# Linear attention and a feed-forward layer in one kernel: the keys' sums added up to 64 partitions before they are spread

## The chip, the cores and the metric

The kernel runs on one core of a Trainium2 chip. The metric is the device time of one execution in microseconds, median of three runs. The core has a matrix engine (TensorE, PE in the profile; its weight loads are PEld), a vector engine (VectorE, DVE), a scalar engine (ScalarE, ACT), GpSimd (POOL) and a queue that issues transfers (SP). They run side by side and wait for each other by semaphores. Each works through its own instructions in the order in which they stand in the program.

## The reference

Random-feature attention for 8 batches, 8 heads, 576 tokens and a head size of 64 with 128 features, and after it a feed-forward layer over all 4608 tokens:

```python
def phi(x):
    proj = np.einsum('bhsd,md->bhsm', x, omega)
    sq = np.sum(x * x, axis=-1, keepdims=True) / 2.0
    h = proj - sq
    h = h - np.max(h, axis=-1, keepdims=True)
    return np.exp(h) / np.sqrt(m)
q_p, k_p = (phi(q_s), phi(k_s))
kv = np.einsum('bhsm,bhsd->bhmd', k_p, v)
z = np.sum(k_p, axis=2)
num = np.einsum('bhsm,bhmd->bhsd', q_p, kv)
den = np.einsum('bhsm,bhm->bhs', q_p, z)[..., None] + 1e-06
...
h = x @ w_in            # x: num / den as 4608 x 512; w_in 512 x 2048
g = h - np.tanh(h)
return g @ w_out        # 2048 x 512
```

The change concerns z, the sum of the keys' features over the tokens.

## The kernel before

The work is cut into units. A k unit takes one batch b and one pair of heads c and makes two things: `kvw`, the product of the keys' features with the values, and `zb`, the sums z of both heads, spread over all 128 partitions. A q unit takes one chunk of 256 tokens and one pair of heads and makes the columns x that the feed-forward layer reads. The feed-forward layer runs over 18 chunks of 256 tokens, in steps `ffn_h` (products with w_in, L469, then tanh, subtraction and a split of g, L473 to L476) and `ffn_out` (products with w_out, L487 to L489). Between the steps a `beat` advances every open unit by one stage, up to its next `yield`. Chunks 0 and 1 run together in the first part; from chunk 2 on one chunk follows the other.

Matrix products in fp32 are made from fp32r parts: a number is split into a rounded part (hi) and the rest (lo), and the products of the parts are added in PSUM.

Batches 0 and 1 take another path. The 24 units of batches 2 to 7 go through `k_single`. There the features `pa`, `pm` and `pb` of the keys (4, 1 and 4 blocks of 128 tokens) are split by `split` into `khl` and multiplied with the split values `vhl` (L268) into the PSUM bank `pk`. Beside that, `zsum` (L271) and L291, L292 add up the features on GpSimd in `zs`, with 128 partitions (tokens modulo 128) by 2 heads by 128 features. What is left is the sum over the partitions: a product with a matrix of ones, which also spreads the result over all partitions. The changed lines prepare that product and issue it.

Order of the work: the program is written stage by stage as above, and a scheduler then places the instructions of all engines by simulated times. A small edit can therefore move instructions far from it. Buffers set waits too. `khl` has two buffers, and `zhl` takes one of them; `c1` has one, shared by `zt` in `zsum` and by the tile `c1` of L299 (the profile prints it as `c`); `pk` has one bank.

The transition matters for the prediction. At L605 to L612 the first part of the feed-forward layer ends, its output tiles are stored (L500), and chunk 2 starts as soon as its x is split (L409). Around that place the units of batch 2 run, 5 beats apart. Their names in the order below are `2_0` to `2_3` or, for tiles, the head pair and the pool's number.

Of the kernel before, what the change touches and what calls it, by code (L numbers as in the profile page):

```python
# [8 lines left out]
F32 = mybir.dt.float32  # L9
F32R = mybir.dt.float32r  # L10
# [7 lines left out]
B, H, S, D, M = 8, 8, 576, 64, 128  # L18
NT, DM, DFF = B * S, H * D, 2048
P = 128  # L20
# [11 lines left out]
def favor_attention_ffn(ctx: ExitStack, tc: tile.TileContext, qT, kT, va, vt, omT, w, out):  # L32
# [12 lines left out]
    nc = tc.nc  # L45
# [18 lines left out]
    def bank(kind):  # L64
        tags = mode[kind]
        tags.append(tags.pop(0))
        return tags[-1]

    def att(kind, shape, dtype, name):
        pool, bufs = mode[kind]  # L70
        return pool.tile(shape, dtype, tag=kind, name=name, bufs=bufs)
# [30 lines left out]
    ones = const.tile([P, P], F32R, name="ones")  # L102
# [22 lines left out]
    def split_rows(x, f):  # L125

        copy(mode["hi"], x[0:D, 0, :], f[0:D])
        copy(mode["hi"], x[D:P, 1, :], f[D:P])
        nc.vector.tensor_sub(x[D:P, 0, :], f[0:D], x[0:D, 0, :].bitcast(F32))
        nc.vector.tensor_sub(x[0:D, 1, :], f[D:P], x[D:P, 1, :].bitcast(F32))  # L130

    def features(lhs, name):

        n = len(lhs)
        ph = att("phi", [P, 4, M], F32, f"phi_{name}")
        nb = sb.tile([P, 4], F32, tag="nb", name=f"nb_{name}", bufs=12)

        for g in range(0, n, 2):
            m = min(2, n - g)
            pj = ps.tile([P, 2, 2 * M], F32, tag=bank("pj"), name=f"pj_{name}_{g}")  # L140
            for i in range(m):
                nc.tensor.matmul(pj[:, i], lhs[g + i], om2, start=True, stop=True)  # L142
            nc.scalar.copy(ph[:, g : g + m], pj[:, :m, M:])  # L143
            for i in range(m):
                j = g + i
                nc.vector.tensor_tensor_reduce(  # L146
                    ph[:, j], pj[:, i, :M], ph[:, j], scale=-SCALE, scalar=3.0e38,
                    op0=ALU.add, op1=ALU.min, accum_out=nb[:, j : j + 1])
        for j in range(n):
            nc.scalar.activation(ph[:, j], ph[:, j], AF.Exp, bias=nb[:, j : j + 1], scale=-1.0)  # L150
        return ph
# [18 lines left out]
    def k_unit(b, c):  # L170

        n = f"{b}_{c}"
        if not mode["native"]:
            f = att("kf", [P, S], F32, f"kf_{n}")
            load(f, kT[c, :, b * S : (b + 1) * S])
            yield from k_single(b, c, f)
            return
# [51 lines left out]
    def k_single(b, c, f):  # L229


        n = f"{b}_{c}"
        v = att("vr", [P, 9, D], F32, f"v_{n}")
        nc.sync.dma_start(v, vt[b - 2, c])
        yield
        x = att("kx", [P, 2, S], F32R, f"kx_{n}")
        split_rows(x, f)
        yield
        xf = x.rearrange("p h s -> p (h s)")
        tiles = [xf[:, t * P : (t + 1) * P] for t in range(9)]  # L240
        pk = ps.tile([P, 2, 2, M], F32, tag=bank("pk"), name=f"pk_{n}")
        zs = att("zs", [P, 2, M], F32, f"zs_{n}")

        def split(ph, t, n_t):

            ku = []
            for g in range(0, n_t, 2):
                w = min(2, n_t - g)
                k = att("khl", [P, 2, 2, M], F32R, f"khl_{n}_{t + g}")
                u = att("vhl", [P, 2, 2, D], F32R, f"vhl_{n}_{t + g}")  # L250
                nc.vector.tensor_copy(k[:, :w, 0], ph[:, g : g + w])  # L251
                nc.gpsimd.tensor_sub(k[:, :w, 1], ph[:, g : g + w], k[:, :w, 0].bitcast(F32))  # L252
                if n_t > 1:
                    parts = [(slice(0, P), slice(0, w), slice(t + g, t + g + w))]
                else:
                    parts = [(slice(D * h, D * h + D), h, t) for h in range(2)]
                    nc.gpsimd.memset(u[0:D, 1].bitcast(F32), 0.0)
                    nc.gpsimd.memset(u[D:P, 0].bitcast(F32), 0.0)
                for p, i, j in parts:
                    nc.gpsimd.tensor_copy(u[p, i, 0], v[p, j])  # L260
                    nc.vector.tensor_sub(u[p, i, 1], v[p, j], u[p, i, 0].bitcast(F32))  # L261
                ku += [(k[:, i if n_t > 1 else 0].rearrange("p a m -> p (a m)"),
                        u[:, i].rearrange("p a d -> p (a d)")) for i in range(2)]
            return ku

        def kv(h, ku, first, last):
            for i, (k, u) in enumerate(ku):
                nc.tensor.matmul(pk[:, h].rearrange("p a m -> p (a m)"), u, k,  # L268
                                 start=first and i == 0, stop=last and i == len(ku) - 1)

        def zsum(ph, h):  # L271
            zt = att("c1", [P, 2, M], F32, f"zt_{n}_{h}")
            nc.gpsimd.tensor_add(zt, ph[:, 0:2], ph[:, 2:4])
            nc.gpsimd.tensor_add(zs[:, h], zt[:, 0], zt[:, 1])

        pa = features(tiles[0:4], f"ka{n}")
        yield
        ku = split(pa, 0, 4)
        zsum(pa, 0)
        yield  # L280
        pm = features(tiles[4:5], f"km{n}")
        kv(0, ku, True, False)
        yield
        km = split(pm, 4, 1)
        yield
        pb = features(tiles[5:9], f"kb{n}")
        kv(0, km[:1], False, True)
        kv(1, km[1:], True, False)
        yield
        zsum(pb, 1)  # L290
        nc.gpsimd.tensor_add(zs[0:D, 0], zs[0:D, 0], pm[0:D, 0])  # L291
        nc.gpsimd.tensor_add(zs[D:P, 1], zs[D:P, 1], pm[D:P, 0])  # L292
        ku = split(pb, 5, 4)
        yield
        kv(1, ku, False, True)
        zhl = att("khl", [P, 2, 2, M], F32R, f"zhl_{n}")
        nc.vector.tensor_copy(zhl[:, 0], zs)
        nc.gpsimd.tensor_sub(zhl[:, 1], zs, zhl[:, 0].bitcast(F32))
        c1 = att("c1", [P, 2, M], F32, f"c1_{n}")  # L299
        nc.scalar.copy(c1, pk[:, :, 0])  # L300
        nc.vector.tensor_add(c1, pk[:, :, 1], c1)
        yield
        for h in range(2):
            nc.tensor.transpose(pk[:, 0, h], c1[:, h], ident)  # L304
        for i in range(2):
            nc.tensor.matmul(pk[:, 1].rearrange("p h m -> p (h m)"), ones,  # L306
                             zhl[:, i].rearrange("p h m -> p (h m)"), start=i == 0, stop=i == 1)
        kvt = att("kvs", [P, 2, D], F32, f"kvs_{n}")
        nc.scalar.copy(kvt, pk[:, 0, :, D:])
        nc.vector.tensor_add(kvt, pk[:, 0, :, 0:D], kvt)  # L310
        zb = att("zb", [P, 2, M], F32, f"zb_{n}")
        nc.scalar.copy(zb, pk[:, 1])
        w = att("kvw", [P, 4, D], F32R, f"kvw_{n}")
        nc.scalar.copy(w[:, 0::3, :], kvt)
        nc.vector.tensor_sub(w[:, 1:3, :], kvt, w[:, 0::3, :].bitcast(F32))
        kvs[b, c] = (w.rearrange("p a d -> p (a d)"), zb)
# [216 lines left out]
    start = {}  # L533
# [54 lines left out]
    start = {}  # L588
# [76 lines left out]
```

## Time and profile before

| | |
|---|---|
| time, median of 3 runs | 1074.74 us (1074.12 to 1076.08) |
| profiled execution | 1074.43 us, span 1072.6 us |
| busy TensorE, VectorE, ScalarE, GpSimd | 1045.6, 853.1, 713.4, 328.5 us |
| mean granted TensorE clock | 0.989 |
| product with the ones, L306 | 48 instructions, 128x256 each |
| cast of the sums, L297 (VectorE) | 24 instructions, 8.0 us |
| rest of the split, L298 (GpSimd) | 24 instructions, 18.0 us |

A row of the profile names line, engine, operation, the tile written and the tiles read. "Idle before" is the time for which an engine did nothing ahead of an instruction, with the instruction that released it. A granted clock of 0.5 means that TensorE ran at half speed.

### The profile page before, as it was taken

The page shows a single profiled execution, that of the slowest core. Times are in us where ns is not written, and L with a number is a line of the kernel's source. Part 1 is how long each engine was busy: PE and PEld are TensorE (multiplying, and loading weights), DVE is VectorE, ACT ScalarE, POOL GpSimd, SP SyncE. Part 2 cuts the span into 40 slices and gives each one's busy share as a digit, 9 for nine tenths or more (in the row PEclk, how much of TensorE's full clock was granted, in tenths as well). Part 3 has the DMA queues.
Part 4 walks back from the last instruction along what each step waited for, and adds up shares of the span by engine and source line. Part 5 has one row for each costly group of instructions (what it writes and reads, how often), then busy time and mean ns, then how long its engine had stood idle before and what let it go on. Part 6 is the DMA issues. An engine that isn't in the chain of part 4 may idle for free. (4 is left out here: it accounts for less than half of the span.)

```text
span 1072.6 us, 20340 instructions
## 1 busy us (share of the span) xinstructions
PE 1045.6 (97%) x6760; PEld 951.3 (89%) x6760; DVE 853.1 (80%) x3028; ACT 713.4 (67%) x1833; POOL 328.5 (31%) x555
## 2 busy tenths in 40 slices
PE   6888999998999999999999999999999999999998
PEld 5777888997999999999999999999999999999997
DVE  5999796898888986688888888898888897666522
ACT  5997565777777765577777766777767775555422
POOL 8534440344433320133333333233333331000000
PEclk8999999998999999999999999999999999999999
DMA  9651401111111110011111111111101110000000
GB/s 296 175 179 60 189 1 36 58 28 53 33 53 33 53 33 30 12 53 33 52 34 43 43 28 53 31 45 33 53 22 52 29 42 11 30 11 26 1 21 20
DMA packets 35530, 55.91 MB, mean 52 GB/s; under 512 B 12256, under 2 KB 21600, under 8 KB 33376
## 3 DMA queue, kind: packets, MB, share of 16 engines
q1 hardware_dynamic: 35344, 54.57, 16.1%
q8 instruction: 54, 0.88, 0.3%
q14 instruction: 52, 0.43, 0.1%
q10 hardware_dynamic: 80, 0.03, 0.0%
HBM read 45.15 MB, written 9.44 MB: 51 GB/s over the span
## 5 line engine op out<-in xcount | busy, mean ns | idle before, releaser
L469 PE MATMUL h<-xh,w 128*128 128x256 f32 (+1 forms) x2176 | 454.2, 292 | 2.1 <-DVE g L474 2.1
L469 PEld LDWEIGHTS h<-xh,w 128*128 128x128 f32 x2176 | 357.1, 191 | 12.0 <-DVE g L474 2.7
L469 PE MATMUL h<-xl,w 128*128 128x256 f32 (+1 forms) x1088 | 317.2, 292 | 0.5 <-DVE xl L409 0.5
L487 PE MATMUL po<-w,gh 128*128 128x512 f32 x544 | 214.1, 394 | 0.0
L469 PEld LDWEIGHTS h<-xl,w 128*128 128x128 f32 x1088 | 207.8, 191 | 6.6 <-DVE xl L409 0.8
L488 PE MATMUL po<-w,gh 128*128 128x512 f32 x544 | 213.7, 393 | 0.0
L489 PE MATMUL po<-w,gl 128*128 128x512 f32 x544 | 210.1, 392 | 0.0
L473 ACT ACTIVATE g<-h 128x512 f32<-128x512 f32 x144 | 85.0, 590 | 96.5 <-PE h L469 89.8
L474 DVE TENSOR_TENSOR g<-h,g 128x512 f32<-128x512 f32 x144 | 98.8, 686 | 60.8 <-ACT g L473 60.0
L475 ACT CAST gh<-g 128x512 fp32r<-128x512 f32 x144 | 89.5, 621 | 85.8 <-DVE g L474 83.4
L476 DVE TENSOR_TENSOR gl<-g,gh 128x512 fp32r<-128x512 f32 x144 | 109.4, 760 | 42.1 <-ACT gh L475 38.7
L489 PEld LDWEIGHTS po<-w,gl 128*128 128x128 f32 x544 | 102.1, 188 | 20.4
L487 PEld LDWEIGHTS po<-w,gh 128*128 128x128 f32 x544 | 102.6, 189 | 16.6 <-ACT gh L475 0.2
L488 PEld LDWEIGHTS po<-w,gh 128*128 128x128 f32 x544 | 102.5, 188 | 15.2
L349 DVE CUSTOM_DVE_ANT_0 junk<-phi_q,zb 128x128 f32<-128x128 f32 (+1 forms) x320 | 95.9, 303 | 14.7 <-ACT phi_q L150 0.8
L252 POOL TENSOR_TENSOR khl<-phi_ka,khl 128x256 fp32r<-128x256 f32 x48 | 38.3, 799 | 155.3 <-DVE khl L251 134.1
L440 POOL TENSOR_SCALAR a<-a 128x1024 f32<-128x1024 f32 x16 | 62.1, 3883 | 67.6 <-ACT a L437 55.7
L150 ACT ACTIVATE phi_q<-phi_q,nb_q 128x128 f32<-128x128 f32 x240 | 79.1, 392 | 4.7 <-DVE nb_q L146 4.5
L260 POOL CAST vhl<-v 128x128 fp32r<-128x128 f32 (+1 forms) x144 | 44.6, 311 | 103.1 <-PE pk L268 78.6
L389 DVE TENSOR_TENSOR ql<-pt,qh 128x512 fp32r<-128x512 f32 x60 | 41.1, 685 | 27.5 <-ACT qh L388 27.2
L146 DVE CUSTOM_DVE_ANT_0 phi_q<-pj_q,phi_q 128x128 f32<-128x128 f32 x240 | 55.8, 283 | 2.8 <-ACT phi_q L143 2.5
L261 DVE TENSOR_TENSOR vhl<-v,vhl 128x128 fp32r<-128x128 f32 (+1 forms) x144 | 44.7, 311 | 16.3 <-POOL vhl L260 12.8
(150 smaller groups left out, 1961.0 us busy)
## 6 DMA issues: line engine op xcount, KB each, us to landing
raw<-w SPq DMA_DIRECT2D x16, 1024.0 KB, 7.2
kf<-kT SPq DMA_DIRECT2D x32, 288.0 KB, 2.9
qf<-qT SPq DMA_DIRECT2D x72, 128.0 KB, 2.1
out<-o SPq DMA_DIRECT2D x36, 256.0 KB, 2.0
v<-vt SPq DMA_DIRECT2D x24, 288.0 KB, 2.9
v<-va SPq DMA_DIRECT2D x8, 288.0 KB, 5.9
omf<-omT ACTq DMA_DIRECT2D x1, 32.0 KB, 2.1
omf<-omT SPq DMA_DIRECT2D x1, 32.0 KB, 2.3
```

The costliest lines, as they stand in the source:

```text
L146: nc.vector.tensor_tensor_reduce(ph[:, j], pj[:, i, :M], ph[:, j], scale=-SCALE, scalar=3.0e38, op0=ALU.add, op1=ALU.min, accum_out=nb[:, ...
L150: nc.scalar.activation(ph[:, j], ph[:, j], AF.Exp, bias=nb[:, j : j + 1], scale=-1.0)
L349: nc.vector.tensor_tensor_reduce(bank("junk")[r], ph[r, i], kvs[b, c][1][r, h], scale=1.0, scalar=EPS, op0=ALU.mult, op1=ALU.add, accum_ou ...
L440: nc.gpsimd.tensor_scalar(a.bitcast(F32), a.bitcast(F32), 2.0**-15, 122879.9921875, op0=ALU.max, op1=ALU.min)
L469: nc.tensor.matmul(o, w_, x, start=i == 0, stop=i == len(prods) - 1)
L473: nc.scalar.activation(g, p, AF.Tanh)
L474: nc.vector.tensor_sub(g, p, g)
L475: nc.scalar.copy(gh, g)
L476: nc.vector.tensor_sub(gl, g, gh.bitcast(F32))
L487: nc.tensor.matmul(po[t], h, wt[f][:, 0, DM:], start=first, stop=False)
L488: nc.tensor.matmul(po[t], h, wt[f][:, 1, DM:], start=False, stop=False)
L489: nc.tensor.matmul(po[t], l, wt[f][:, 0, DM:], start=False, stop=last)
```

## The change

Before, `zs` is split on all 128 partitions into a hi and a lo part, and two products with the ones add both up. Now the upper 64 partitions are first added to the lower 64: ScalarE copies them down, GpSimd adds. ScalarE then writes the hi part of that sum on partitions 0 to 63 of `zhl`, and VectorE the lo part on partitions 64 to 127. One product with the ones sums all 128 partitions, hi and lo together. The tile for the halves, `zt`, is taken from `c1`.

```diff
         kv(1, ku, False, True)
-        zhl = att("khl", [P, 2, 2, M], F32R, f"zhl_{n}")
-        nc.vector.tensor_copy(zhl[:, 0], zs)
-        nc.gpsimd.tensor_sub(zhl[:, 1], zs, zhl[:, 0].bitcast(F32))
+
+        zt = att("c1", [P, 2, M], F32, f"zh_{n}")
+        nc.scalar.copy(zt[0:D], zs[D:P])
+        nc.gpsimd.tensor_add(zt[0:D], zs[0:D], zt[0:D])
+        zhl = att("khl", [P, 2, M], F32R, f"zhl_{n}")
+        nc.scalar.copy(zhl[0:D], zt[0:D])
+        nc.vector.tensor_sub(zhl[D:P], zt[0:D], zhl[0:D].bitcast(F32))
         c1 = att("c1", [P, 2, M], F32, f"c1_{n}")
         nc.scalar.copy(c1, pk[:, :, 0])
         nc.vector.tensor_add(c1, pk[:, :, 1], c1)
         yield
         for h in range(2):
             nc.tensor.transpose(pk[:, 0, h], c1[:, h], ident)
-        for i in range(2):
-            nc.tensor.matmul(pk[:, 1].rearrange("p h m -> p (h m)"), ones,
-                             zhl[:, i].rearrange("p h m -> p (h m)"), start=i == 0, stop=i == 1)
+        nc.tensor.matmul(pk[:, 1].rearrange("p h m -> p (h m)"), ones,
+                         zhl.rearrange("p h m -> p (h m)"), start=True, stop=True)
```

Lines behind the change move by 3: L469 becomes L472, L349 becomes L352, L304 and L306 become L308 and L309. The numbers at the ends of names are the built program's own and differ between the two.

TensorE at the transition: unit 2_1's transposes and products with the ones, and what stands behind them, up to the product of unit 2_2 that waits at 244 us. Before:

```order
L304 MATMUL pk_1_2163<-ident,c_2_1_2512 128x128 x2
L306 MATMUL pk_1_2163<-zhl_1_2509,ones 128x256 x2
L142 MATMUL pj_km_2_0_2593<-om,kx_2_2410 128x256
L469 MATMUL h_1_2873<-xh,w_326 128x256
L469 MATMUL h_1_2873<-xl,w_326 128x256
L469 MATMUL h_1_2873<-xh,w_326 128x256
L395 MATMUL pn_3_2634<-qh_3_2587,kvw_3_996 128x256
L396 MATMUL pn_3_2634<-ql_3_2588,kvw_3_996 128x256
L142 MATMUL pj_kb_2_0_2677<-om,kx_2_2410 128x256 x2
L142 MATMUL pj_kb_2_2_2683<-om,kx_2_2410 128x256 x2
```

And now:

```order
L308 MATMUL pk_1_2163<-ident,c_2_1_2517 128x128 x2
L309 MATMUL pk_1_2163<-zhl_1_2514,ones 128x256
L142 MATMUL pj_km_2_0_2597<-om,kx_2_2412 128x256
L398 MATMUL pn_3_2638<-qh_3_2591,kvw_3_996 128x256
L399 MATMUL pn_3_2638<-ql_3_2592,kvw_3_996 128x256
L142 MATMUL pj_kb_2_0_2681<-om,kx_2_2412 128x256 x2
L142 MATMUL pj_kb_2_2_2687<-om,kx_2_2412 128x256 x2
```

The three feed-forward products that stood between have moved ahead of the transposes; up to the last row TensorE has the same work as before, less one product with the ones in each of the two units.

VectorE at the same place, up to the minimum of unit 2_2 (`nb_km`) that releases that last product (the ISA rows are the sums for the denominators and the minima). Before:

```order
L130 TENSOR_TENSOR qx_1_2704<-qf_1_2655,qx_1_2704 64x256
L349 ISA junk,dn_0_2548<-phi_q_0_2530,zb_0_750 128x128
L349 ISA junk,dn_0_2548<-phi_q_0_2530,zb_0_2261 128x128
L251 CAST khl_2_2_2521<-phi_ka_2_2450 128x2x128
L352 RECIPROCAL dn_0_2548<-dn_0_2548 128x4
L310 TENSOR_TENSOR kvs_1_2574<-pk_1_2163,kvs_1_2574 128x128
L146 ISA phi_km_2_2591,nb_km_2_2592<-pj_km_2_0_2593,phi_km_2_2591 128x128
L358 TENSOR_SCALAR phi_q_0_2530<-phi_q_0_2530,dn_0_2548 128x128 x3
```

And now:

```order
L130 TENSOR_TENSOR qx_1_2708<-qf_1_2659,qx_1_2708 64x256
L251 CAST khl_2_2_2526<-phi_ka_2_2452 128x2x128
L352 ISA junk,dn_0_2553<-phi_q_0_2535,zb_0_750 128x128
L352 ISA junk,dn_0_2553<-phi_q_0_2535,zb_0_2263 128x128
L313 TENSOR_TENSOR kvs_1_2578<-pk_1_2163,kvs_1_2578 128x128
L146 ISA phi_km_2_2595,nb_km_2_2596<-pj_km_2_0_2597,phi_km_2_2595 128x128
L355 RECIPROCAL dn_0_2553<-dn_0_2553 128x4
L404 TENSOR_TENSOR xs_3_2644<-pn_3_2638,tmp_3_2643 64x256
```

The cast stands earlier, and the reciprocal has moved behind the minimum.

ScalarE in a later unit, 3_0, from the queries' projections to the copy of `pk` into c1 (`c_3_0`). Before:

```order
L143 COPY phi_q_1_3645<-pj_q_1_2_3653 128x256
L75 CAST qx_2_3799<-qf_2_3775 64x256 x2
L388 CAST qh_0_3575<-pt_0_3570 128x512
L150 ACTIVATE phi_q_1_3645<-phi_q_1_3645,nb_q_1_3646 128x128 x4
L300 COPY c_3_0_3567<-pk_0_3272 128x256
L473 ACTIVATE g_0_3615<-h_0_3590 128x512
```

And now:

```order
L75 CAST qx_2_3809<-qf_2_3775 64x256 x2
L298 COPY zh_0_3572<-zs_0_3281 64x256
L150 ACTIVATE phi_q_1_3655<-phi_q_1_3655,nb_q_1_3656 128x128 x4
L301 CAST zhl_0_3575<-zh_0_3572 64x256
L391 CAST qh_0_3586<-pt_0_3581 128x512
L304 COPY c_3_0_3578<-pk_0_3280 128x256
L359 ACTIVATE phi_q_1_3655<-phi_q_1_3655,dn_1_3673 128x128
L476 ACTIVATE g_0_3626<-h_0_3601 128x512
```

The two new instructions, `zh` and `zhl`, stand ahead of the copy into c1, with the exponentials of a q unit between them.

## The prediction

> **What bounds the kernel now.** I read the page's engine totals first, then TensorE over four long stretches, then its waits, then single instructions around the place that the change touches. The totals and the stretches (busy time and number of instructions of each engine, then the granted clock):
>
> ```profile
> PE 1045.6 (97%) x6760; PEld 951.3 (89%) x6760; DVE 853.1 (80%) x3028; ACT 713.4 (67%) x1833; POOL 328.5 (31%) x555
> ...
> 204.00:241.00 37.00, 37.00 (x247) 33.69 (x246) 34.25 (x124) 27.16 (x75) 17.33 (x30) 1.00 0.14 40
> 242.00:244.40 2.40, 0.54 (x3) 0.37 (x3) 2.19 (x12) 1.28 (x6) 0.51 (x1) 1.00 0.46 157
> 260.00:300.00 40.00, 40.00 (x277) 36.94 (x276) 34.88 (x140) 27.71 (x77) 15.38 (x32) 1.00 0.10 26
> 300.00:900.00 600.00, 599.21 (x4096) 555.36 (x4095) 511.56 (x1997) 423.60 (x1135) 200.35 (x386) 1.00 0.13 38
> ```
>
> From 260 us to 900 us, where 21 of the 24 units that the change touches finish, TensorE idles 0.8 us in all. There a matmul that is taken away should be time taken away. What one is worth is read from start to start, because matmuls overlap and their own durations count the overlap twice:
>
> ```profile
> 218.60 0.39 PE L487 MATMUL po<-w,gh 128*128 128x512 f32 x1
> 218.83 0.38 PE L304 MATMUL pk<-ident,c 128*128 128x128 f32 x2
> 218.96 0.49 PE L306 MATMUL pk<-zhl,ones 128*128 128x256 f32 x2
> 219.29 0.39 PE L488 MATMUL po<-w,gh 128*128 128x512 f32 x1
> 219.52 0.39 PE L489 MATMUL po<-w,gl 128*128 128x512 f32 x1
> 219.75 0.28 PE L469 MATMUL h<-xh,w 128*128 128x256 f32 x1
> 219.87 0.28 PE L469 MATMUL h<-xl,w 128*128 128x256 f32 x1
> ...
> L306 PE MATMUL pk<-zhl,ones x48: 277/323/369, 219.0 to 900.6; 128*128 128x256 f32 x48
> ```
>
> A product of 256 columns holds TensorE for 0.12 us (219.75 to 219.87), one of 512 columns for 0.23 us (219.29 to 219.52). The two transposes and two products with the ones take 218.83 to 219.29 = 0.46 us: two of 0.11 and two of 0.12, so no switching cost hides there. The median "duration" of 323 ns is nearly three times what a product costs.
>
> One place differs. Between the last feed-forward step of the first two token chunks and the first of chunk 2, TensorE waits for VectorE, and the clock falls:
>
> ```profile
> PE pj_kb L142 <- DVE nb_km L146: 1.8, 1, 1.8
> PE pk L304 <- DVE c L301: 0.3, 1, 0.3
> ...
> 244.33 0.76 PE L142 MATMUL pj_kb<-om,kx 128*128 128x256 f32 x2 [1.79 <-DVE nb_km L146]
> 250.40 0.58 PE L469 MATMUL h<-xl,w 128*128 128x256 f32 x1 [0.51 <-DVE xl L409]
> ...
> 243.52 0.29 DVE L251 CAST khl<-phi_ka 128x256 fp32r<-128x256 f32 x1
> 243.72 0.17 DVE L352 RECIPROCAL dn<-dn 128x4 f32<-128x4 f32 x1
> 243.81 0.26 DVE L310 TENSOR_TENSOR kvs<-pk,kvs 128x128 f32<-128x128 f32 x1
> 243.99 0.28 DVE L146 CUSTOM_DVE_ANT_0 phi_km<-pj_km,phi_km 128x128 f32<-128x128 f32 x1
> ...
> 244.00:248.00 4.00, 2.91 (x11) 0.55 0.25 89
> 248.00:252.00 4.00, 3.49 (x15) 0.50 0.31 70
> 252.00:256.00 4.00, 4.00 (x27) 0.67 0.35 120
> 256.00:260.00 4.00, 4.00 (x32) 1.00 0.00 0
> ```
>
> The last four rows are TensorE alone (busy, instructions, clock). VectorE's instructions follow each other without a gap up to 243.99, so it is VectorE's backlog that releases TensorE; after the idle time the granted clock is about half for 10 us. The low clock costs roughly 2.91 x 0.45 + 3.49 x 0.50 + 4.00 x 0.33 = 4.4 us on top of the idle time. Units 2_0 and 2_1 (first batch of the split path, head pairs 0 and 1) finish before this stall.
>
> **The change, part by part.** Durations for the added instructions come from instructions of the same engine and shape, and the removed ones stand in the trace:
>
> ```profile
> L297 DVE CAST zhl<-zs x24: 279/295/718, 212.6 to 895.9; 128x256 fp32r<-128x256 f32 x24
> L298 POOL TENSOR_TENSOR zhl<-zs,zhl x24: 732/739/972, 212.9 to 896.2; 128x256 fp32r<-128x256 f32 x24
> L75 ACT CAST qx<-qf x120: 401/404/417, 166.6 to 988.2; 64x256 fp32r<-64x256 f32 x120
> L129 DVE TENSOR_TENSOR qx<-qf,qx x60: 418/419/704, 167.4 to 989.0; 64x256 fp32r<-64x256 f32 x60
> L300 ACT COPY c<-pk x24: 347/370/394, 214.4 to 896.2; 128x256 f32<-128x256 f32 x24
> L301 DVE TENSOR_TENSOR c<-pk,c x24: 406/416/424, 217.2 to 896.7; 128x256 f32<-128x256 f32 x24
> ```
>
> TensorE loses one product in each of 24 units: 24 x 0.12 = 2.88 us. The Trainium skill, "TensorE: Matmul & The Clock Gate", section Back-to-back issue gap, gives N/2.4 + 2.5 ns for a warm matmul alone, an estimate of 109 ns at 256 columns; by it the term would be 2.6 us. The trace's spacing of 0.12 us is what is used.
>
> VectorE exchanges a cast (295 ns) for a subtraction of 64x256 (419 ns): +0.12 us a unit, 3.0 us in all. From 300 to 900 us it is busy 511.56 of 600 us, so some 88 us of idle time cover that; if that cover were gone, as it is just before 244 us, the price would be 0.12 us a unit on the path.
>
> ScalarE gains two instructions of 64x256, 2 x 0.404 = 0.81 us a unit, 19.4 us in all. Its 176 us of idle time in the same stretch hide them. Without cover they would delay the tanh and the cast of g behind them in its queue.
>
> GpSimd exchanges a subtraction over 256 columns (739 ns) for an addition over 256 columns on 64 partitions. No row has that shape; the bounds are 454 ns (below) and 739 ns, and I take 739, since the row with the same 256 columns is nearest. It is busy a third of the time, so both ends cost nothing by themselves:
>
> ```profile
> L292 POOL TENSOR_TENSOR zs<-zs,phi_km x24: 454/790/912, 209.8 to 895.0; 64x128 f32<-64x128 f32 x24
> ```
>
> The new wait is longer. From finished sums to both parts took 0.30 + 0.74 = 1.03 us on two engines; now it is 0.40 + 0.74 + 0.40 + 0.42 = 1.97 us over four hand-offs. The copy of pk into c1 and the addition behind it used to run beside this; now c1's only buffer holds zt, so they wait for the last subtraction: 1.97 + 0.37 + 0.42 = 2.75 us before the transposes may start. For the first unit in the trace, L292 starts at 209.8 and the transposes at 218.83, so the cover there is 7 us or more. The last unit has 895.0 to its product with the ones at 900.6, 5.6 us, which covers L292's own 0.8, the 2.75, and the transposes. Between 0 (the cover holds everywhere) and 0.3 us a unit (the one unit where the transposes already waited for c) I take 0 for most of them and keep 24 x 0.05 = 1.2 us, some four such waits, for the range. Queued behind a held subtraction on VectorE are the subtractions of g, whose readers are the output products.
>
> Before the stall the saving is lost: TensorE reaches its waiting place 2 x 0.12 = 0.24 us earlier and waits that much longer. When the stall ends is set by VectorE. One of its two casts before the stall was a slow one:
>
> ```profile
> 232.72 0.72 DVE L297 CAST zhl<-zs 128x256 fp32r<-128x256 f32 x1
> ```
>
> The two subtractions cost 2 x 0.42 against 0.29 + 0.72, -0.17 us, or 2 x 0.12 = +0.25 us if the slowness stays and hits the successor too; and the reciprocal (0.17 us) now stands behind the minimum that TensorE waits for. The bounds are -0.34 and +0.1; I take 0, between them.
>
> Sum: -2.88 + 0.24 + 0 = -2.6 us. The profiled execution took 1074.43 us (span 1072.6 and 1.8 around it), which becomes 1071.8; it lay 0.3 under the median of 1074.74, so the forecast is 1072.1 us. Own range: 1071.5 (the stall ends 0.34 earlier and TensorE's 0.3 for the late c goes) to 1073.4 (the stall 0.1 later and the 1.2 of new waits).
>
> **The rivals.** (1) Gain eaten. Every 0.1 us by which a transpose waits for its c1 takes a unit's saving. It needs 0.1 us on average; for it speaks that the chain is 0.9 us longer and now serial with c1, against it that the order puts the transposes later behind the last product of their unit. Time: 1074.5.
>
> (2) A shorter slow stretch. If VectorE's backlog at 244 us is smaller (its cast of 0.72 us has a successor that takes 0.42 undisturbed) and the clock comes back a third of the 10 us earlier, 3.4 x 0.5 = 1.7 us are gained, and up to 1.5 us of idle time: 1072.1 - 1.7 to 1072.1 - 3.2, centre 1069.6. Against it: the low clock came back only when TensorE had worked without a gap for some 4 us after 250.4 (the row of L469 above is its last wait there), and that is paced by VectorE, whose work there is the same.
>
> (3) Slower: the new subtraction holds VectorE's queue in the stretch before 244 us, where VectorE works 34.25 of 37 us. It waits for ScalarE, which waits for GpSimd, which waits for ScalarE. The trace has one such hold at the old place:
>
> ```profile
> ACT g L473 <- DVE zhl L297: 1.4, 1, 1.4
> DVE zhl L297 <- POOL zs L292: 1.3, 2, 0.9
> ```
>
> If both units before the stall hold VectorE 1.4 us, the idle time of TensorE grows by 2.8 us, and a further half-clock stretch of 3.4 us adds 1.7: 1072.1 + 4.5 = 1076.6. It decides the sign from 2.6 us lost, and can be told from no change from 4.8 us. Against it: VectorE itself waited for the sums only 1.3 us in two of 24 units (second row). A version of it in which the clock loses nothing further ends at 1072.1 + 2.8 = 1074.9; I give that 0.03 of rival 3's chance, since the clock did fall here after idle time of 1.79 us.
>
> The Trainium skill, "TensorE: Matmul & The Clock Gate", section Why this matters for your kernels, says that only idle gaps over about 3 us throw the clock back to half. By that rule rival 3 would be its milder version. The trace disagrees: the longest gap before 244.33 was 1.79 us, and the clock still fell.
>
> **How the numbers follow.** Chances: forecast 0.50, gain eaten 0.19, shorter slow stretch 0.14, slower 0.17 (0.03 of it in the milder version). I call 0.2% (2.15 us) what a measurement can tell from no change. The forecast's 2.6 us lies little above that, so of its 0.50 I count 0.36 as faster and 0.14 as same; with rival 2, faster is 0.50. Same is 0.14, 0.17 of rival 1 and the 0.03: 0.34. Slower is 0.14 of rival 3 and 0.02 of rival 1: 0.16. The range goes from 1069.0, inside rival 2, to 1076.6, the centre of rival 3, and leaves about 0.07 on either side.
>
> **What would show it.** In the changed profile: the product with the ones 24 times; the wait of L142 for nb_km still about 1.8 to 2.1 us and the half clock 10 us long; TensorE idle under 1.5 us between 260 and 900; the last feed-forward product of the span about 2.6 us earlier. Wrong would be: TensorE waiting for c in many units, a second stretch of half clock, or the one after 244 us gone or longer by a third.

## The result and the profile after

The changed kernel takes 1089.26 us (median of 4 runs, 1088.56 to 1090.48) against 1075.41 us for the kernel before on the same chip (4 runs, 1074.12 to 1076.45). The ratio is 1.0127, with an interval from 1.0112 to 1.0142: 13.7 us slower. The forecast of 1072.1 us and its range up to 1076.6 us were both missed. The profiled execution took 1088.81 us (span 1087.0).

Engine totals of the changed kernel, and its stretches (PE, PEld, DVE, ACT, POOL busy with the number of instructions, granted clock, share of the DMA engines, GB/s):

```profile
PE 1051.2 (97%) x6736; PEld 949.8 (87%) x6736; DVE 865.2 (80%) x3028; ACT 731.3 (67%) x1881; POOL 326.0 (30%) x555
...
204.00:241.00 37.00, 36.23 (x241) 32.81 (x240) 33.78 (x126) 27.82 (x76) 17.34 (x30) 1.00 0.14 40
242.00:244.40 2.40, 1.46 (x9) 0.94 (x7) 2.17 (x12) 2.33 (x8) 1.04 (x2) 1.00 0.06 22
260.00:300.00 40.00, 39.37 (x267) 36.08 (x266) 34.87 (x131) 27.42 (x76) 16.30 (x32) 1.00 0.08 23
300.00:900.00 600.00, 592.68 (x3991) 543.86 (x3991) 510.46 (x1958) 430.23 (x1154) 192.19 (x380) 1.00 0.13 38
```

TensorE has its 24 products less (6760 to 6736 instructions). But from 300 to 900 us it gets through 3991 instructions instead of 4096. About 20 of the 105 are the products that no longer exist; the other 85, at 600/4096 = 0.146 us each, are 12.4 us of lost progress, nearly the whole loss. VectorE is as busy as before (510.5 against 511.6 us) with 39 instructions less: its work has become longer. Only 7.2 us of idle time show on TensorE between 260 and 900 us more than before. The rest does not show as idle time, since a matmul's recorded duration (291 ns on average for the feed-forward products) is longer than the 0.12 us between two starts and covers a short wait.

So I also measured the waits from start to start. From 255 to 925 us, every instruction of TensorE is allowed 0.113 us, or 0.231 us with 512 columns, and what the next start lies later is counted for the next instruction, if it is more than 0.01 us. Before, that gives 13.8 us in all; now 28.7. The products of keys and values (L268) account for 0.7 us before and 6.4 now, the transposes of phi_q (L365, now L368) for 3.3 and 5.6, the first feed-forward products for 4.6 and 6.5, the output products for 1.0 and 5.9.

The loss is spread over the whole stretch, but not evenly. By the timeline, the transposes of the unit that started them at 264.1 us before now start 2.6 us later. At 396.7 us they are 7.2 us late, at 504.4 us 7.8 us, at 560.4 us 9.4 us and at 900.2 us 15.3 us.

The changed lines themselves, from the costliest groups of the changed kernel (busy us in all and mean ns of one; then the idle time of the engine before them and what ended it):

```profile
L299 POOL TENSOR_TENSOR zh<-zs,zh 64x256 f32<-64x256 f32 x24 | 18.1, 753 | 13.3 <-ACT zh L298 11.0 <-PE pk L268 1.8 <-PE h L472 0.5
L302 DVE TENSOR_TENSOR zhl<-zh,zhl 64x256 fp32r<-64x256 f32 x24 | 10.0, 418 | 0.8
L298 ACT COPY zh<-zs 64x256 f32<-64x256 f32 x24 | 9.7, 405 | 19.2 <-POOL zs L292 18.7
L301 ACT CAST zhl<-zh 64x256 fp32r<-64x256 f32 x24 | 9.7, 403 | 3.2 <-POOL zh L299 2.8
L304 ACT COPY c<-pk 128x256 f32<-128x256 f32 x24 | 8.8, 367 | 3.6 <-DVE zhl L302 3.4
L309 PE MATMUL pk<-zhl,ones 128*128 128x256 f32 x24 | 8.7, 364 | 0.0
```

Each instruction takes as long as forecast (0.40, 0.74, 0.40, 0.42 us). What was not in the sum stands in the right-hand column: ScalarE stands still 18.7 us for the sums, 2.8 us for the addition and 3.4 us for the subtraction, and GpSimd 11.0 us for the copy. VectorE is not held: ahead of its subtraction it stands idle for 0.8 us in all 24 units together. The product with the ones itself, the reader of the chain, waits for nothing.

The place at 244 us is not where the time went. TensorE alone in four stretches (busy, instructions, clock):

```profile
244.00:248.00 4.00, 1.87 (x11) 1.00 0.32 98
248.00:252.00 4.00, 2.69 (x11) 0.51 0.24 74
252.00:256.00 4.00, 4.00 (x25) 0.64 0.53 143
256.00:260.00 4.00, 4.00 (x35) 1.00 0.12 33
...
PE pj_kb L142 <- DVE nb_km L146: 2.0, 1, 2.0
```

(The last line is from TensorE's waits.) Busy time multiplied by the clock gives 1.87 + 1.37 + 2.56 + 4.00 = 9.8 us of work, against 1.60 + 1.75 + 2.68 + 4.00 = 10.0 from the rows of before. TensorE idles more and the clock falls later: by these rows it is at half speed for 6.8 us instead of 10.2. Together the two change 0.2 us.

A picture of one wait that is new, at 348 us in the changed kernel (start, duration, engine, line):

```profile
348.23 0.26 DVE L251 CAST khl<-phi_ka 128x256 fp32r<-128x256 f32 x1
348.29 0.80 POOL L273 TENSOR_TENSOR zt<-phi_ka 128x256 f32<-128x256 f32 x1 [6.78 <-ACT phi_ka L150]
348.40 2.14 DVE L361 TENSOR_SCALAR phi_q<-phi_q,dn 128x128 f32<-128x128 f32 x3
...
349.05 1.42 POOL L252 TENSOR_TENSOR khl<-phi_ka,khl 128x256 fp32r<-128x256 f32 x2
350.47 0.68 DVE L477 TENSOR_TENSOR g<-h,g 128x512 f32<-128x512 f32 x1
350.60 0.44 PE L368 MATMUL pt<-ident,phi_q 128*128 128x128 f32 x2 [0.34 <-DVE phi_q L361]
351.18 0.62 ACT L478 CAST gh<-g 128x512 fp32r<-128x512 f32 x1 [2.09 <-DVE g L477]
```

And the same pieces of the same unit in the kernel before:

```profile
343.40 0.68 DVE L358 TENSOR_SCALAR phi_q<-phi_q,dn 128x128 f32<-128x128 f32 x3
344.19 0.49 DVE L251 CAST khl<-phi_ka 128x256 fp32r<-128x256 f32 x2
344.56 0.74 POOL L252 TENSOR_TENSOR khl<-phi_ka,khl 128x256 fp32r<-128x256 f32 x1 [7.70 <-DVE khl L251]
344.67 0.69 DVE L474 TENSOR_TENSOR g<-h,g 128x512 f32<-128x512 f32 x1
```

Before, the scaling of phi_q (three instructions) ran ahead of the split of the next unit's keys and took 0.68 us. Now the split stands first, GpSimd starts on its part, and the same three instructions take 2.14 us beside it. The transposes of phi_q wait for them, g stands behind them, and ScalarE waits 2.09 us for g. The same picture returns at 514.6 and 860.1 us (2.16 us for the three) and, milder, at 543.8 and 675.3 us (1.68 and 1.87 us). None of the chain's own steps is in it; what is new in it is the order of the others.

### The profile page after: what moved, and what is told of

It reads as the page before. It is cut to its first block, busy times and chain, and to the rows that moved or that the text cites. A ratio compares the mean times of both kernels' runs of the same rounds, so it can differ in the third digit from the quotient of the medians.

```text
span 1087.0 us, 20295 instructions
## 1 busy us (share of the span) xinstructions
PE 1051.2 (97%) x6736; PEld 949.8 (87%) x6736; DVE 865.2 (80%) x3028; ACT 731.3 (67%) x1881; POOL 326.0 (30%) x555
## 4 chain that ended last, share of the span: by engine, by line
PE 47%; DVE 13%; ACT 5%; POOL 3%; issue 3%; DMA 0%; DVEq 0%; POOLq 0%; ACTq 0%
PE h L472 20%; PE po L490 7%; PE po L491 6%; PE po L492 6%; DVE junk L352 2%; PE pj_q L142 1%; PE pt L368 1%; PE pk L268 1%; DVE gl L479 1%; DVE phi_q L361 1%; DVE g L477 1%; POOL khl L252 1%; PE pn L399 1%; PE pn L398 1%; DVE phi_q L146 1%
## 5 line engine op out<-in xcount | busy, mean ns | idle before, releaser
L472 PE MATMUL h<-xh,w 128*128 128x256 f32 (+1 forms) x2176 | 453.1, 291 | 3.9 <-DVE g L477 3.9
L472 PEld LDWEIGHTS h<-xh,w 128*128 128x128 f32 x2176 | 356.6, 191 | 14.5 <-DVE g L477 5.0
L472 PE MATMUL h<-xl,w 128*128 128x256 f32 (+1 forms) x1088 | 317.1, 292 | 0.5 <-DVE xl L412 0.5
L472 PEld LDWEIGHTS h<-xl,w 128*128 128x128 f32 x1088 | 207.7, 191 | 7.5 <-DVE xl L412 1.0
L476 ACT ACTIVATE g<-h 128x512 f32<-128x512 f32 x144 | 85.0, 591 | 61.4 <-PE h L472 54.5
L352 DVE CUSTOM_DVE_ANT_0 junk<-phi_q,zb 128x128 f32<-128x128 f32 (+1 forms) x320 | 96.6, 305 | 15.2 <-ACT phi_q L150 0.8
L361 DVE TENSOR_SCALAR phi_q<-phi_q,dn 128x128 f32<-128x128 f32 x204 | 58.2, 340 | 1.1
```

Of the source, the lines that this page charges most:

```text
L352: nc.vector.tensor_tensor_reduce(bank("junk")[r], ph[r, i], kvs[b, c][1][r, h], scale=1.0, scalar=EPS, op0=ALU.mult, op1=ALU.add, accum_ou ...
L361: e.tensor_scalar(ph[:, i], ph[:, i], dn[:, i : i + 1], 1.0, op0=ALU.mult, op1=ALU.mult)
L472: nc.tensor.matmul(o, w_, x, start=i == 0, stop=i == len(prods) - 1)
L476: nc.scalar.activation(g, p, AF.Tanh)
```

## The experiments

All ratios are against the kernel before, run beside it on the same chip, with a 95% interval; "us" behind a ratio is its distance from 1 times 1076. "By starts" means the count from start to start above, from 255 to 925 us. The letters of theories hold for the text in which they stand.

**A hold or a load on ScalarE alone.** To the kernel before, an unread copy is added, behind the sums or from a constant:

```diff
+        zx = att("zx", [P, 2, M], F32, f"zx_{n}")
+        nc.scalar.copy(zx[0:D], zs[D:P])                       # e1
+        nc.scalar.copy(zx[0:D].rearrange(...), om2[D:P]...)    # e2 instead
```

> The kernel before, with one more instruction per unit: ScalarE copies the upper half of zs (64x256) to a spare tile that nobody reads, so its queue has to wait for GpSimd's last addition. Held-queue theory: the 17 us lost in the changed kernel (14.4 measured and 2.9 that TensorE should have gained) come from ScalarE being held there (18.7 us in 14 waits), so this run loses much of it: 1084 to 1092 us, ScalarE idle 10 us or more ahead of the copy. Rival of the longer serial chain (c1 shared, four hand-offs): the path to the product is as before, so about 1075. Rival of the rearranged order: any size between, with the idle time of ScalarE not ahead of this copy.

> Control for the run with the copy of zs: the same ScalarE copy (64x256, partitions 64 to 127 to 0 to 63) at the same place in the program, but from a constant tile, so it waits for no one. Held-queue theory: 1074 to 1077 us, the 0.4 us of work per unit is hidden. Rival of ScalarE's load: 24 x 0.4 = 9.7 us at most, up to 1085. Rival of the rearranged order: as far from 1075 as the run with the copy of zs.

Measured: 1.0008 (0.9998 to 1.0017) and 0.9990 (0.9981 to 1.0000). ScalarE stood 14.7 us for the sums in the first, nearly as long as in the changed kernel, and it cost 0.9 us. Neither ScalarE's load nor its first stop is the cause by itself.

**Two repairs of the changed kernel.** ScalarE's copy and cast go to VectorE (e3); the halves get a buffer of their own instead of c1 (e4):

```diff
-        nc.scalar.copy(zt[0:D], zs[D:P])          # e3, and the cast likewise
+        nc.vector.tensor_copy(zt[0:D], zs[D:P])
-        zt = att("c1", [P, 2, M], F32, f"zh_{n}") # e4
+        zt = att("zx", [P, 2, M], F32, f"zh_{n}")
```

> The changed kernel with the copy down and the cast of the sums on VectorE instead of ScalarE; one product as in the changed kernel. Held-queue theory, with ScalarE the queue that matters: most of the loss goes, 1071 to 1078 us. Held-queue theory in a wider form (whichever in-order engine waits is the one that loses): VectorE is held, 1085 or more. Rival of the serial chain: the chain is nearly as long (0.3 + 0.7 + 0.3 + 0.4 us), 1085 to 1089.

> The changed kernel, with a buffer of its own for the tile of the halves instead of the only buffer of c1, so that the copy of pk into c1 needn't wait for the last subtraction. Held-queue theory: the hold on zs stays, 1085 to 1090 us. Rival of the serial chain: the transposes come earlier and most of the loss goes, 1072 to 1078.

Measured: 1.0067 (1.0052 to 1.0082) and 1.0056 (1.0038 to 1.0074). Each gives back about half, and each leaves 6 us or more. Both times, 1084.3 and 1083.1 us, lie between the cases that the texts expected.

**The product's worth, the product doubled, the wait of c1, and khl's buffer.**

```diff
-        for i in range(2):                         # e5, on before: hi part only
+        for i in range(1):
-        nc.tensor.matmul(pk[:, 1]..., zhl..., start=True, stop=True)   # e6, on after
+        for i in range(2):
+            nc.tensor.matmul(pk[:, 1]..., zhl..., start=i == 0, stop=i == 1)
+        zq = att("c1", [P, 2, M], F32, f"zq_{n}")  # e7, on before
+        nc.scalar.copy(zq, zs)
-        nc.gpsimd.tensor_sub(zhl[:, 1], zs, zhl[:, 0].bitcast(F32))
+        nc.gpsimd.tensor_sub(zhl[:, 1], zq, zhl[:, 0].bitcast(F32))
-        zhl = att("khl", [P, 2, M], F32R, f"zhl_{n}")  # e8, on after
+        zhl = att("zy", [P, 2, M], F32R, f"zhl_{n}")
```

> The kernel before with only the product of the rounded part; the lo part of the sums is still computed and left out of z. It measures what a product with the ones is worth with the chain as it was. The prediction's first term expects 24 x 0.12 = 2.9 us less (ratio 0.9973). If the product is worth less than it takes on TensorE, because VectorE paces these stretches, the ratio stays above 0.999.

> The changed kernel with its one product issued twice into the same accumulation (z comes out doubled), so that TensorE has the work of before and only the chain ahead of it is new. If the longer chain costs some 17 us and the product saved 2.9, this run is at 1.015 to 1.016 of the time before; if TensorE waits in these stretches anyway, the second product fills waits and it stays at 1.0127.

> The kernel before, both products and the old split, with one thing added: ScalarE copies the sums into a tile of the c1 buffer, and the subtraction on GpSimd reads that copy. So the copy of pk into c1 has to wait for the lo part of the sums, as in the changed kernel, without the other steps. Theory T (the longer serial chain in front of the transposes makes the unit late, and the work bunches on VectorE): 3 to 8 us slower, ratio 1.003 to 1.008, transposes some 1 us later behind the last product of their unit. Rival O (the loss comes from the new kinds of work and where they land, VectorE's subtraction and its collisions with GpSimd): within 0.1% of before, as the copy alone on ScalarE cost nothing.

> The changed kernel with zhl in a buffer of its own, so that the split of the next unit's keys need not wait until the product with the ones has read zhl; the halves still lie in c1. Theory T with the late release of khl as a part of it: 3 us or more of the 14 come back, ratio 1.010 or less. If the transposes behind c1 are what is late, it stays at 1.0127.

Measured: e5 0.9956 (0.9944 to 0.9968), e6 1.0064 (1.0052 to 1.0076), e7 1.0005 (0.9997 to 1.0014), e8 1.0085 (1.0072 to 1.0098).

- e5: a product less is worth 4.7 us (3.4 to 6.0), somewhat more than the 2.9 of the forecast. By starts TensorE's waits fall from 13.8 to 12.0 us, so 1.8 of the 4.7 are waits that went with the new order and 2.9 are left for the product. The gain is real and the chain has eaten it and more.
- e6 surprised: with a second product, that is with more work, the changed kernel is 6.8 us faster. Neither expectation had that. The added instruction makes the scheduler place others differently: some 800 of VectorE's 3028 instructions stand in another order than in the changed kernel. So 7 to 10 us of the loss (the 6.8, and up to 2.9 for the added products) hang on the order in which the instructions happened to fall, and a repair of this kernel that brings 4 to 8 us (e3, e4, e8) proves little by itself. The kernel before stayed within 1.1 us under the edits e1, e2 and e7.
- e7: theory T falls, and rival O's forecast holds. The transposes start 5.4 us behind the end of the last product of their unit instead of 4.4 (median of the 24 units; in the changed kernel 6.0), and it costs 0.5 us. That the transposes come later is not what costs.
- e8: 4.5 us come back, as theory T expected. After e6 and e7 this cannot be told from a mere change of order.

**The steps without a reader, and the fold left out.** e9 keeps the old path complete and adds the four steps in a tile that nobody reads. e10 is the changed kernel without the fold.

```diff
+        zx = att("zx", [P, 2, M], F32, f"zx_{n}")       # e9, on before
+        nc.scalar.copy(zx[0:D], zs[D:P])
+        nc.gpsimd.tensor_add(zx[0:D], zs[0:D], zx[0:D])
+        nc.scalar.copy(zx[0:D], zx[0:D])
+        nc.vector.tensor_sub(zx[0:D], zs[0:D], zx[0:D])
-        nc.scalar.copy(zt[0:D], zs[D:P])                # e10, on after;
-        nc.gpsimd.tensor_add(zt[0:D], zs[0:D], zt[0:D]) # cast and subtraction read zs[0:D]
```

> The kernel before, complete, plus the four steps of the fold (copy on ScalarE, addition on GpSimd, second copy on ScalarE, subtraction on VectorE) in a spare tile that nobody reads. The steps load and hold the queues of the three engines, but nothing waits for them. Theory H (what costs is that the in-order queues of ScalarE, GpSimd and VectorE are held by the hand-offs, the second stop of ScalarE above all, whoever reads the result): 7 us or more slower, ratio 1.007 or more. Theory D (what costs is that the product, the transposes and the buffers stand behind the longer chain): within 0.2% of before, at most 1.002.

> The changed kernel without the copy and the addition: the upper 64 partitions of the sums are left out, and the chain is only the cast on ScalarE and the subtraction on VectorE, with one product. If the two extra hand-offs of the fold cost all of it (H or D alike), the gain of one product shows: ratio 0.996 to 0.998. If the kind and place of the split cost (VectorE behind ScalarE at the end of the chain), it stays above 1.003.

Measured: e9 1.0114 (1.0099 to 1.0129), 12.3 us; e10 0.9995 (0.9985 to 1.0004). This decides against theory D: nothing waits for the dead steps, no buffer of the old path is shared with them, and 12 of the 14 us are there. What is left is what the steps do in the queues in which they stand: they hold them, they load them, and they change the order of the rest (some 1800 of VectorE's 3028 old instructions stand in another order than before). e9 does not tell these apart. e9's waits around the steps from 255 to 925 us, and its stretch from 300 to 900 us:

```profile
ACT zx L300 <- POOL zs L292: 16.9, 17, 1.9
...
POOL zx L301 <- ACT zx L300: 9.8, 17, 1.6
...
ACT zx L302 <- POOL zx L301: 7.1, 13, 1.0
...
PEld pk L268 <- POOL khl L252: 5.2, 12, 1.0
DVE zx L303 <- ACT zx L302: 5.2, 5, 1.2
...
300.00:900.00 600.00, 593.06 (x4004) 544.23 (x4002) 514.26 (x1976) 427.86 (x1153) 213.96 (x398) 1.00 0.13 38
```

Three engines stop in turn, VectorE too, and TensorE's keys-and-values products wait for khl's lo part on GpSimd (12 times, 5.2 us on the weight loads). By starts, those products lose 7.8 us here, 6.4 in the changed kernel and 0.7 in the kernel before; the output products, which lose 5.9 us in the changed kernel, lose only 1.8 here. So e9 has nearly the same loss, but not at the same places. e10 recovers the time, but shows no gain from its product, which neither of its two cases expected. By starts its waits are 16.4 us, 2.6 more than before, 2.2 of them at the transposes of phi_q, which is nearly the product's 2.9. What makes them was not tried apart; its VectorE still waits 4.5 us for the cast on ScalarE, which the kernel before had not.

**Two folds on GpSimd.** GpSimd writes the upper half of the sums to the lower partitions while it adds them up, which needs no copy on ScalarE but one addition more; the copy of pk into c1 stands behind or ahead (e12):

```diff
-            nc.gpsimd.tensor_add(zs[:, h], zt[:, 0], zt[:, 1])
+            if h == 0:
+                nc.gpsimd.tensor_add(zs[0:D, h], zt[0:D, 0], zt[0:D, 1])
+                nc.gpsimd.tensor_add(zx[0:D, h], zt[D:P, 0], zt[D:P, 1])
+            else: ...
-        nc.gpsimd.tensor_add(zs[D:P, 1], zs[D:P, 1], pm[D:P, 0])
+        nc.gpsimd.tensor_add(zx[0:D, 1], zs[D:P, 1], pm[D:P, 0])
-        nc.scalar.copy(zt[0:D], zs[D:P])
```

> A fold without ScalarE's copy: GpSimd writes the upper half of the sums to partitions 0 to 63 of a tile of its own while it adds them up (one addition more per unit, early), and the final addition follows in its own queue, without a hand-off; then the cast on ScalarE, the subtraction on VectorE and one product as in the changed kernel. Under H, ScalarE stops once instead of twice: about half of the 8 us comes back, ratio 0.999 to 1.004. Under D, the chain is 0.7 us shorter and c1 is not shared: 0.997 to 1.003. If GpSimd's extra addition matters (keys' lo parts behind it in the same queue), above 1.005.

> The same with the copy of pk into c1 and its addition written ahead of the last addition, cast and subtraction, so that ScalarE's copy of pk is not queued behind the cast and the transposes do not wait for the sums. Under D better than the run before by 1 us or more; under H the same as that run within 0.1%. A ratio of 0.998 or less would beat the kernel before.

Measured: 1.0135 (1.0119 to 1.0152) and 1.0126 (1.0108 to 1.0144). Both forecasts by H and D failed; the third case of the text held. The order around c1 makes no difference. Against e10, these kernels differ by two additions on GpSimd a unit and the tile for them, and they are 14 to 15 us slower. By starts, L268 loses nothing in them and the transposes of phi_q lose 12.4 and 12.3 us: the same loss at another reader.

**The dead steps one by one.** e13 is e9 with the first two steps, e14 with the first three, and e15 is e9 with the addition on VectorE. e16 is a real fold that gives GpSimd no instruction more and has ScalarE copy early, off the chain:

```diff
+        nc.scalar.copy(zx[0:D, 0], zs[D:P, 0])     # e16, on after, behind zsum(pa, 0)
-        nc.gpsimd.tensor_add(zs[D:P, 1], zs[D:P, 1], pm[D:P, 0])
+        nc.gpsimd.tensor_add(zx[0:D, 1], zs[D:P, 1], pm[D:P, 0])
+        nc.vector.tensor_add(zx[0:D], zs[0:D], zx[0:D])
+        nc.vector.tensor_copy(zhl[0:D], zx[0:D])
+        nc.gpsimd.tensor_sub(zhl[D:P], zx[0:D], zhl[0:D].bitcast(F32))
```

> The kernel before plus two dead steps, the copy on ScalarE (which alone cost nothing) and the addition on GpSimd behind it. Theory G (GpSimd is the place: the addition waits for the copy and stands in front of the lo parts of the values and keys, which the products of L268 wait for): most of the 12 us, ratio 1.006 or more, and the products of L268 late. Theory S (the second stop of ScalarE, which waits for GpSimd, and VectorE's wait behind it): within 0.2% of before.

> The same plus the second copy on ScalarE, that is the dead chain without VectorE's subtraction. Theory G: within 0.2% of the run before this. Theory S with ScalarE as the place: 1.006 or more here and nothing in the run before. If VectorE's subtraction, held behind ScalarE, is the place: within 0.2% of before here, since only the full chain had it.

> The full dead chain with the addition on VectorE instead of GpSimd (0.42 instead of 0.74 us; VectorE gets 0.84 us of work a unit, and ScalarE stops twice as before). Theory G: at most 1.004. Theory S: 1.006 or more, since both stops remain and VectorE is held twice.

> A real fold with one product: ScalarE copies the upper half of the first head's sums down early, GpSimd writes that of the second head to the lower partitions in the addition that it does anyway, and then VectorE adds the halves and makes the rounded part in one stretch of its queue; the lo part is made on GpSimd as in the kernel before. Nothing shares c1. Theory G: GpSimd has as much work as before, so the gain of one product (4 us by e5) comes through less 1 to 2 us for VectorE's 0.42 us a unit: ratio 0.997 to 0.999. Theory S: the same, as ScalarE makes no stop. If VectorE's load is what counts, 1.002 or more.

Measured: e13 1.0081 (1.0066 to 1.0095), e14 1.0052 (1.0040 to 1.0065), e15 1.0112 (1.0099 to 1.0126), e16 0.9991 (0.9981 to 1.0001). The copy alone cost 0.9 us, with GpSimd's addition 8.7 us, with ScalarE's second copy 5.6 us (less, so 3 us are most likely a matter of order again), and with VectorE's subtraction 12.3 us. Theory G alone falls with e15: without GpSimd, but with VectorE behind ScalarE twice, it is 12.1 us. Theory S alone falls with e13. e16 keeps the product's gain only in part: 1 us faster, at the edge of what can be told from no change. But it folds with one product and with no more instructions on GpSimd than the changed kernel has, and is 14.6 us faster than that.

**Load without a wait.** One dead instruction for which its engine waits no longer than it does already:

```diff
+        nc.gpsimd.tensor_add(zx[0:D], zs[0:D], zs[0:D])   # e17, on before
+        nc.vector.tensor_sub(zx[0:D], zs[0:D], zs[0:D])   # e18, on before
```

> The kernel before plus one dead addition of 64x256 on GpSimd in each unit that waits for no other engine (17.7 us of GpSimd in all, as in e13). Load: as e13, ratio 1.006 or more. Hold (the wait for ScalarE in front of it): within 0.2% of before.

> The kernel before plus one dead subtraction of 64x256 on VectorE in each unit, without a new wait (10 us of VectorE in all). Load: 3 us or more, ratio 1.003 or more, as the 0.42 us a unit in e16 and the last step of e9. Hold: within 0.2% of before.

Measured: e17 1.0065 (1.0052 to 1.0078), e18 1.0012 (1.0002 to 1.0022). So 16.6 us of GpSimd, on an engine that is busy 31% of the time, cost 7.0 us, though the addition itself waits for no other engine. 14.4 us of VectorE, which is busy 80%, cost 1.3 us (the subtraction took 0.60 us on average, not the 0.42 expected). The load case held for GpSimd and failed for VectorE.

Of all the runs that lost much, e17 is the one in which the order can't be the reason. By the names in the trace, the instructions of TensorE (6760), ScalarE (1833) and GpSimd (555, without the added ones) follow each other as in the kernel before, and so do all but one of VectorE's 3028. What GpSimd's load does shows on VectorE, in the cast L297 (minimum, median and maximum ns; first and last start) and in the lo part of the values, L261; the last row is L261 in the kernel before:

```profile
L297 DVE CAST zhl<-zs x24: 278/630/722, 213.4 to 903.6; 128x256 fp32r<-128x256 f32 x24
...
300.00:900.00 600.00, 597.12 (x4059) 550.92 (x4058) 517.43 (x1993) 420.37 (x1126) 209.59 (x400) 1.00 0.13 39
...
L261 DVE TENSOR_TENSOR vhl<-v,vhl 128x128 fp32r<-128x128 f32 (+1 forms) x144 | 50.7, 353 | 21.8 <-POOL vhl L260 17.8
...
L261 DVE TENSOR_TENSOR vhl<-v,vhl 128x128 fp32r<-128x128 f32 (+1 forms) x144 | 44.7, 311 | 16.3 <-POOL vhl L260 12.8
```

The same cast had a median of 295 ns before. It is the same instruction on the same tile; in 13 of the 24 units the added addition now runs beside it and it takes 0.57 us or more. VectorE is busy 5.9 us longer from 300 to 900 us with 4 instructions less. This does not cost TensorE evenly: its transposes with c1 are 2.1 us late at the unit of 264.1 us, 2.8 at 616.5 and 7.8 at 900.2, though seven of the slowed casts stand before 616 us. Behind 616 us the waits by starts grow by 4.8 us, 1.9 of them at the transposes of phi_q and 1.9 at L268.

## Why the prediction was wrong

- **The product, -2.88 us:** right. e5 measured -4.7 (-3.4 to -6.0), of which 1.8 are waits that went with the new order.
- **The place at 244 us, +0.24 and 0:** right to 0.2 us of work, by luck, since it expected neither the longer idle time nor the shorter stretch at half clock, and the two nearly cancel. Rivals 2 and 3 both put the decision there, and it was not there. Rival 2's shorter slow stretch came (6.8 instead of 10.2 us), but not its gain.
- **VectorE, +0.12 us a unit, hidden:** as a load, right. e18 put 0.60 us a unit there for 1.3 us in all.
- **ScalarE, +0.81 us a unit, hidden:** right for half of it as a load (e2), and right for the first stop (e1).
- **GpSimd, "both ends cost nothing by themselves":** the reason given, that it is busy a third of the time, fails. In this change one instruction of 0.74 us takes another's place, so no load was added; but e17 shows that 0.69 us a unit costs 7.0 us with the order kept, and so the idle share of GpSimd is no cover.
- **The new wait, taken as 0, with 24 x 0.05 = 1.2 us kept for the range:** this is the step that failed. The term is 13.7 + 2.9 = 16.6 us, or 18.4 with e5's 4.7 for the product; by starts, TensorE's waits grow by 14.9 us between 255 and 925 us. The working asked whether the chain's readers, the transposes and the product, would wait, found 5.6 to 7 us of cover for them, and this was true: e7 shows that transposes 1 us later cost nothing, and the product waits for nothing. The cover is that of the chain's readers. What has no cover is the other work in the queues in which the chain's steps stand, which they hold and push into another order. The prediction named a part of it ("the subtractions of g, whose readers are the output products") and gave it no price. By starts the output products account for 4.9 of the 14.9 us, of which 1.4 are one wait for ScalarE's copy of an output tile (L503, at 891 us). The largest part, 5.7 us, lies at the keys-and-values products (L268), which the prediction did not name.
- **Rival 1, gain eaten by transposes that wait for c1:** not what happened. TensorE was held up for c by more than 0.1 us once, for 0.4 us, and once before, for 0.5.
- **Rival 3, slower at 1076.6:** right in sign, but not in its mechanism. It let the new subtraction hold VectorE's queue in the two units before 244 us. In the changed kernel VectorE stood idle ahead of that subtraction for 0.8 us in all 24 units; the queues that were held are those of ScalarE and GpSimd, over the whole stretch. The dead chain e9 did hold VectorE there, for 5.2 us in 5 units, but so did e10, which is no slower than the kernel before, for 4.5 us in 9.

What the 17 to 18 us consist of, as far as the runs go: the four steps in their queues without readers 12.3 us (e9). Step by step the copy adds 0.9, the addition behind it 7.8, the second copy -3.1, the subtraction 6.7; a step that takes 3 us off shows that these are not prices of the steps alone. The addition's part can't be carried over whole, since the changed kernel gives up a subtraction of the same length on GpSimd. The c1 buffer is worth up to 7.6 us in the changed kernel (e4), and its wait 0.5 us when it is added to the kernel before (e7). All of these contain the scheduler's new order, which e6 shows to be worth 7 to 10 us by itself; only e17 kept the old one. The collisions with GpSimd are not enough for an explanation either: of the scalings of phi_q from 255 to 925 us, 12 of 144 took longer than 0.45 us before and 26 of 141 in the changed kernel, but also 24 of 144 in e10, which is no slower than the kernel before. How the sum divides between the hold of ScalarE and GpSimd, the collisions and the order of placement stays open; no run kept the order and changed the chain. What is shown is that the loss needs no reader of the steps (e9), and that a kernel without the fold (e10), or with one that keeps ScalarE's steps out of the end of the chain (e16), is back at the time before, though without most of the product's gain.

## What to carry to other kernels

When a chain is made longer, ask of each hand-off what stands behind the waiting instruction in its queue and where the others move, for every unit and not for one place; the slack of the chain's reader is no cover for those. The idle share of an engine covers work on it only if nobody waits for its results soon and it slows no neighbour: here the engine that was 31% busy was the dearer one (e17) and the one that was 67% busy was free (e2). Where a scheduler places by simulated times, set a repair that gains a few microseconds beside an edit that should gain nothing: one that only added work made the changed kernel 6.8 us faster. And see whether the order of the instructions stayed: where it did, as in e17, the difference belongs to the edit itself.

## What the hardware showed

VectorE is slowed beside GpSimd, depending on where its operands lie. In the kernel before, from 255 to 925 us, the subtraction gl (L476, both operands in SBUF) took 0.69 us on average without GpSimd beside it (54 times) and 0.96 us, up to 1.25, when GpSimd worked for at least 80% of its time (31 times). The subtraction g of the same size (L474), which reads h from PSUM, took 0.69 us both ways (41 and 44 times). The cast of khl on 128x256 (SBUF to SBUF) took 0.29 us (31 times) and 0.51 (16 times), the scaling of phi_q 0.28 (121 times) and 0.66 (13 times). The Trainium skill, "SBUF — State Buffer", section Who interferes with whom, says that VectorE and GpSimd share one pair of ports, that an instruction with two SBUF inputs, a cast or a scaling with a scalar can contend for it, and that one with at most one SBUF input outside the two-port modes doesn't. The trace agrees, with 0.69 against 0.96 us for the one and 0.69 both ways for the other.
